# The first phase of a recurrent attention kernel, put in another order

## The chip, the cores and the metric

The kernel runs on one core of one Trainium2 chip. A core has five engines that run side by side, each through its own list of instructions in order: TensorE (PE, matmuls), VectorE (DVE), ScalarE (ACT), GpSimd (POOL), and SyncE (SP), which here does nothing but start DMAs. Engines wait for each other and for DMAs through semaphores. The metric is device time of one launch in microseconds, as the median of several runs.

## What is computed

Two layers in one launch. The first is a recurrence over time with a 40 x 40 state for each of 32 heads (4 batches of 8), over 768 positions; the second is a feed-forward layer with a bent square as its activation, on the 3072 rows that come out:

```python
for t in range(S):
    y[:, :, t] = np.einsum('bhd,bhde->bhe', rt, state)
    Sa = np.einsum('bhde,bhe->bhd', state, at)
    state_decay = state * wt[:, :, None, :] - np.einsum('bhd,bhe->bhde', Sa, bt)
    state = state_decay + np.einsum('bhd,bhe->bhde', vt, kt)
...
h = x @ w_in                       # 3072 x 320 by 320 x 2048
g = np.where(pos, h, np.where(neg, 0.0, (h + beta) ** 2 / (4.0 * beta)))
return g @ w_out                   # 3072 x 2048 by 2048 x 320
```

Inputs and results are float32; the weights come to the kernel as 64-bit integers whose two words together hold the double-precision number.

## The kernel before

**The recurrence in chunks.** 768 positions are 24 chunks (`c`) of 32, and each chunk has two halves (`hb`) of 16 heads. Inside a chunk the recurrence becomes small matrix products, one of which needs the inverse of a 32 x 32 triangular matrix per head. Four chunks make a set (`s`), of which there are six; a set's decay products, its scores and its inverses are worked out together.

**What a set needs before its chunks can run:**

- *Pair products* (`early_products` for sets 0 and 1, `prelude` for the later ones): running products of the decays and what follows from them, on VectorE and POOL. They leave `early_out[s]`, which lies in the buffers `wides[1]` for set 0 and `wides[0]` for set 1.
- *Rows in memory*: `early_store` writes these products, and `copy_rv` with `pad_scr` copies the inputs r and v, to a scratch tensor `scr[s]`. From it `load_ti` and `load_cg` (part 0) fetch the rows of one chunk half into `tih[hb]` and `cg`.
- *Scores for the inverse*: `early_turn` transposes the products with TensorE, and ScalarE copies them to `turned[s]`; `early_ab` multiplies them, copies the result (L206) and stores it to `abd[s]` in eight DMAs (L208).
- *The inverse* (`invert`): L316 loads `abd[s]` into `lw`; then 31 pairs of a multiply (L326) and a subtraction (L332), each dependent on the one before, on VectorE for set 0 and on POOL for later sets; L335 stores the inverse to `ttd[s]`, and `load_cg` part 1 (L409) fetches it for a chunk half. `step_back("inv", 0)` issues one further step of it.

**The chain of chunks.** `chain(c, hb)` begins with the matmuls of L463 and takes five steps (matmuls L463, L473, L491, transposes L520, matmuls L529, with VectorE and ScalarE work between them). `turn` transposes rows on VectorE, and `scores` works out in-chunk scores. The main loop calls `step` ten times for each chunk, alternating between halves. In the text a step is one such call, counted from the loop's start: chunk 1 begins at step 10, chunk 2 at step 20. With each step go two `pull(wgen, 2)` resumptions of the weight conversion, a piece of feed-forward work (`feed`), and the share of the later sets' preparation that is due by then (`background`, by the step windows in `WINDOWS`: the inverse of set 1 from step 16 to 36, the rows of set 2 from step 20 to 36).

**The feed-forward layer** (`moe`) works on groups of 64 positions, 12 in all. Group 0 is laid out after step 21 of the main loop, and its work is let in with a delay of five steps. A group goes through 16 blocks `f` of 128 hidden units; block `f` needs columns of `w_in` and rows of `w_out`. Its matmuls are L600, L574 and L578.

**The weight conversion** (`weights`, a generator called `wgen`) turns the 64-bit numbers into pairs of rounded floats. There are 28 jobs: 12 for `w_in` (`into`, 1024 words wide in the buffer) and 16 for `w_out` (`outof`, 640 words). A job has a load, a scaling on ScalarE (L681), three instructions on VectorE (L687, L716, L718), a cast on ScalarE (L694) and the split-off of the rest on POOL (L695). Two resumptions of the generator issue about one job. The raw numbers stay in lent buffers: `lending` lists which kinds may be used (5 and 6 are the two X tiles, 7 `lw`, 8 `arena`, 9 `tiab`, and before the change 1 for the two `tih` tiles and 2 for `Yraw`). `reclaim(kind)` takes a kind back: it resumes the generator until no job stands in it.

**The first phase** is everything ahead of the main loop. All DMAs in question stand in SP's one list, in the order in which the program issues them. Before the change the phase runs: loads for sets 0 and 1, first weight loads, products of set 0, transposes of set 0, products of set 1, weight loads and conversions between the two halves of the scores, the inversion of set 0. While the inversion's 62 instructions are issued one a step (`i`), a table `todo` adds other work at given `i`, and `rest` adds one DMA a step: stores of set 0, copies of r and v, stores of set 1. At every fifth `i` the conversion is resumed once.

Of the kernel before, what the change touches and what calls it, by code (L numbers as in the profile page):

```python
# [10 lines left out]
F32R = mybir.dt.float32r  # L11
# [38 lines left out]
def rwkv_moe_kernel(ctx: ExitStack, tc: tile.TileContext, r, k, v, w, a, b, w_in, w_out, ident_d, mask_d, out):  # L50
    nc = tc.nc
# [68 lines left out]
    def copy_rv(s, part, c):  # L120

        x, o = ((r, O_R), (v, O_V))[part]
        nc.sync.dma_start(
            scr4[s][c, :, :, o : o + D], x.rearrange("b h (n t) e -> (b h) n t e", t=L)[:, 4 * s + c]
        )

    def pad_scr(s):
        nc.sync.dma_start(scr[s][NH * 128 : NH * 128 + 1, 0:D], r[0, 0, 0:1, :])
# [6 lines left out]
    early_in = [[x.rearrange("p (t e) -> p t e", e=D) for x in xs] for xs in early_in]  # L135
    early_out = [x.rearrange("p (t x) -> p t x", x=160) for x in (wides[1], wides[0])]
    turned = [
        [cgf[i][:, 0:2048].rearrange("p (n t) -> p n t", t=L) for i in ij] for ij in ((0, 1), (2, 0))
    ]

    early_rows = {}
# [7 lines left out]
    def early_products(s):  # L149

        wl, al, bl, kl = early_in[s]
        R = early_out[s]
        kt, P, at, bt = (R[:, :, D * i : D * i + D] for i in range(4))
        rec = arena.rearrange("p (t e) -> p t e", e=D)
        seg = lambda x: x.rearrange("p (s t) e -> p s t e", t=8)
        Ps, ws, rs = seg(P), seg(wl), seg(rec)
        nc.vector.tensor_copy(Ps[:, 1:, 0], ws[:, 1:, 0])
        nc.vector.tensor_scalar(out=P[:, 0], in0=wl[:, 0], scalar1=-1.0, scalar2=None, op0=ALU.mult)
        for t in range(1, 8):
            nc.vector.tensor_mul(Ps[:, :, t], Ps[:, :, t - 1], ws[:, :, t])  # L160
        for i in range(1, 4):
            nc.vector.tensor_mul(Ps[:, i], Ps[:, i], Ps[:, i - 1, 7:8].broadcast_to([128, 8, D]))
        nc.gpsimd.tensor_scalar(out=at[:, 0], in0=al[:, 0], scalar1=-1.0, scalar2=None, op0=ALU.mult)
        for i in range(4):
            ts_ = slice(max(8 * i, 1), 8 * i + 8)
            nc.gpsimd.tensor_mul(at[:, ts_], al[:, ts_], P[:, max(8 * i, 1) - 1 : 8 * i + 7])
        nc.vector.reciprocal(rs[:, :, 7], Ps[:, :, 7])
        for t in range(7, 0, -1):
            nc.vector.tensor_mul(rs[:, :, t - 1], rs[:, :, t], ws[:, :, t])
        for i in range(4):  # L170
            ts_ = slice(8 * i, 8 * i + 8)
            nc.vector.tensor_mul(bt[:, ts_], bl[:, ts_], rec[:, ts_])
        for h in range(2):
            ts_ = slice(16 * h, 16 * h + 16)
            nc.gpsimd.tensor_mul(kt[:, ts_], kl[:, ts_], rec[:, ts_])

    def early_turn(s, j, part):

        for i in range(2):
            ps = psum().rearrange("p (t n) -> p t n", n=128)  # L180
            at = 8 * part + 4 * i
            for k in range(4):
                nc.tensor.transpose(ps[0:D, k, :], early_out[s][:, at + k, 80 + 40 * j : 120 + 40 * j], eye)
            for f in range(2):
                nc.scalar.copy(
                    turned[s][j][64 * f : 64 * f + D, :, at : at + 4].rearrange("e (p c) t -> e p c t", c=4),
                    ps[0:D].rearrange("e t (p f c) -> e f p c t", f=2, c=4)[:, f],
                )
# [24 lines left out]
    def early_store(s, c):  # L213

        nc.sync.dma_start(scr4[s][c, :, :, 80:240], early_out[s][c::4])
# [403 lines left out]
    def weights():  # L619
# [18 lines left out]
        def outof(f):  # L638
            ready_at[f] = len(jobs) + 1
            jobs.append(  # L640
                ([w_out[128 * f : 128 * f + 128, :]], f // 8, lambda f=f: (w2[f // 8][:, 0, f % 8], w2[f // 8][:, 1, f % 8]))
            )

        for j in range(4):
            into(j)
        for f in range(8):
            outof(f)
        for f in range(8, NF):
            outof(f)
        todo = list(range(len(jobs)))  # L650
        size = lambda k: (sum(x.shape[0] for x in jobs[k][0]), jobs[k][0][0].shape[1])

# [72 lines left out]
    def reclaim(kind):  # L725

        lending.discard(kind)
        while any(x[0] == kind for x in sts.values()):
            next(wgen)

    def pull(gen, n=1):
        for _ in range(n):
            if next(gen, "end") == "end":
                return False
        return True

    ready_in, ready_at, converted, w2 = {}, {}, [0], []
    needs = lambda f: max(ready_in[f], ready_at[f])
    lending, sts, room, loader = {1, 2, 5, 6, 7, 8, 9}, {}, [], []
    load = lambda q: loader[0](q)  # L740
    pair = lambda x: x.rearrange("p (a b) -> p a b", b=2)
    wgen = weights()
# [1 line left out]
    def step_back(key, s):  # L744
        if s < NS and done.get(key, -1) < s:
            next(back[key])
# [3 lines left out]
    for f in range(2):  # L750
        nc.sync.dma_start(ident[64 * f : 64 * f + 64], ident_d[64 * f : 64 * f + 64, 64 * f : 64 * f + D])
    nc.sync.dma_start(mask, mask_d)
    lend = lambda n, xs: room.extend((n, x.bitcast(I32)) for x in xs)
    lend(5, [Xraw[0]])
    lend(6, [Xraw[1]])
# [2 lines left out]
    for j in range(2):  # L758
        for k in range(4):
            early_turn(0, j, k)  # L760
    early_products(1)
    lend(1, [flat(x) for x in (tih[1], tih[0])])
    lend(9, [flat(tiab)])
    lend(8, [arena])
    load(nc.sync)
    pull(wgen, 2)
    early_ab(0, 0)
    pull(wgen, 2)
    early_ab(0, 1)
    step_back("inv", 0)  # L770
    lend(2, [Yraw])
    load(nc.sync)
    pull(wgen, 2)
    rest = []
    for c in range(4):
        rest += [lambda c=c: early_store(0, c)] + [lambda c=c, i=i: copy_rv(0, i, c) for i in range(2)]
    rest += [lambda: pad_scr(0)]
    rest += [lambda c=c: early_store(1, c) for c in range(4)]
    i = 0
    todo = {}  # L780
    at = lambda n, f: todo.setdefault(n, []).append(f)

    def reuse():

        reclaim(1)
        for x in tih:
            pad_rows(x, 168)
        for hb in range(2):
            load_ti(0, hb)
            load_cg(0, hb, (0,))  # L790

    def ahead(hb):
        for j in range(3):
# [4 lines left out]

    for j in range(2):
        for k in range(4):  # L800
            at(1 + 4 * j + k, lambda j=j, k=k: early_turn(1, j, k))
    at(9, lambda: early_ab(1, 0))
    at(10, lambda: early_ab(1, 1))
    at(14, lambda: w2.append(wide(1)))
    at(24, lambda: w2.append(wide(0)))
    for k in range(3):
        at(12 + 2 * k, lambda k=k: init_cg(k, 0))
        at(16 + 2 * k, lambda k=k: init_cg(k, 1))
    at(3, lambda: lending.discard(1))
    at(16, reuse)  # L810
    at(36, lambda: lending.discard(2))
    at(51, lambda: ahead(0))
    at(55, lambda: ahead(1))
    while done.get("inv", -1) < 0:
        step_back("inv", 0)
        i += 1
        for f in todo.pop(i, ()):
            f()
        if rest:
            rest.pop(0)()  # L820
        if i % 5 == 0:
            pull(wgen)
    assert not todo, todo
    lend(7, [lw])
    load(nc.sync)
    reclaim(2)
    Y.append(y_tile(F32R))
    for hb in range(2):
        load_cg(0, hb, (1,))
    jobs_done = [0]  # L830
    mgen = moe()
    gens = {}
# [107 lines left out]
```

## Time and profile before

| | us |
|---|---|
| median of 3 runs | 1017.51 |
| lowest and highest run | 1013.65, 1018.44 |
| the profiled execution | 1022.44 |
| its span, first to last instruction | 1020.6 |
| busy in the span: PE, POOL, DVE, ACT | 809.8, 583.5, 564.4, 529.9 |
| first chain matmul (L463) starts | 116.58 |
| granted TensorE clock, mean | 0.844 |

Times in the profile are microseconds from the span's start, durations in means are in ns. A group of instructions is named by line, engine and operation, with what it writes and reads. "Idle before" is time in which the engine waited just ahead of such an instruction, with the releaser. SPq rows are the issues of DMAs on SP. A busy engine may be one that stands in the middle of an instruction and is held up there, so equal instructions are compared by duration too.

### The profile page before, as it was taken

Reading aid. Unit: us, or ns where it says so; the run is one execution under the profiler, and the core shown is the slowest. Engines: PE = TensorE matmul, PEld = TensorE weight load, DVE = VectorE, ACT = ScalarE, POOL = GpSimd, SP = SyncE. Lnnn points to the kernel's source line nnn. Section 1 sums busy time; section 2 is a strip of 40 time slices with the busy share of each in tenths; the row PEclk is TensorE's granted clock in tenths of the full one; section 3 lists DMA queues with packets and bytes.
Section 4 is the critical chain, followed back from the end, with each engine's and each line's share of the span. In section 5 each row is a group of like instructions: output and inputs, shape, how many; then the busy total and the mean of one; then the engine's idle time right before and its main releaser. Section 6 shows DMA issues by size and latency. Waiting matters only on the chain.

```text
span 1020.6 us, 34597 instructions
## 1 busy us (share of the span) xinstructions
PE 809.8 (79%) x14240; PEld 725.4 (71%) x14240; DVE 564.4 (55%) x1432; ACT 529.9 (52%) x1326; POOL 583.5 (57%) x781
## 2 busy tenths in 40 slices
PE   4511375556988977899879898989999899999995
PEld 3311365445877966788778787868998789999995
DVE  7598388464555662774643675654554345455321
ACT  5671254213554543564455455546666466667663
POOL 4423354687452699543699544798346984434332
PEclk9755555667797889797888898989999899999998
DMA  6699694755587755885735885755755355443010
GB/s 249 165 216 234 160 220 103 167 109 127 128 172 142 157 135 118 165 174 124 165 87 111 180 172 123 154 122 119 134 115 116 85 105 89 111 77 73 12 43 14
DMA packets 276862, 134.56 MB, mean 132 GB/s; under 512 B 194984, under 2 KB 266856, under 8 KB 276704
## 3 DMA queue, kind: packets, MB, share of 16 engines
q1 hardware_dynamic: 273504, 121.20, 55.6%
q0 software_dynamic: 3200, 11.14, 3.6%
q8 instruction: 112, 1.84, 0.8%
q14 instruction: 46, 0.38, 0.1%
HBM read 96.83 MB, written 33.82 MB: 128 GB/s over the span
## 4 chain that ended last, share of the span: by engine, by line
PE 36%; POOL 19%; DMA 11%; DVE 9%; issue 8%; SPq 7%; ACT 4%; POOLq 0%; DVEq 0%; ACTq 0%
PE ph L600 11%; PE po L574 6%; POOL lw L326 5%; POOL lw L332 5%; DMA ti<-scr 4%; PE po L578 4%; PE p L473 3%; PE p L491 3%; POOL gl L588 3%; DMA ld_a<-in_a_dram 3%; POOL cg L447 3%; PE p L463 3%; SPq L274 2%; PE p L435 2%; DVE arena L243 2%
## 5 line engine op out<-in xcount | busy, mean ns | idle before, releaser
L600 PE MATMUL ph<-X,w 120*128 120x256 f32 x1536 | 263.1, 309 | 23.2 <-DVE qt L613 17.9
L588 POOL TENSOR_TENSOR gl<-qt,gh 128x256 fp32r<-128x256 f32 x192 | 140.4, 731 | 236.6 <-ACT gh L587 215.9
L600 PEld LDWEIGHTS ph<-X,w 120*128 120x128 f32 x1536 | 223.1, 206 | 39.3 <-DVE qt L613 21.4
L613 DVE SCALAR_TENSOR_TENSOR qt<-qt,ph 128x256 f32<-128x256 f32 x192 | 79.9, 416 | 172.5 <-ACT qt L607 166.3
L574 PE MATMUL po<-wide,gh 128*128 128x320 f32 x768 | 165.1, 332 | 0.4 <-ACT gh L587 0.4
L587 ACT CAST gh<-qt 128x256 fp32r<-128x256 f32 x192 | 78.0, 406 | 163.4 <-DVE qt L613 162.6
L447 POOL TENSOR_TENSOR cg<-cg,mask 32x512 f32<-32x512 f32 x96 | 121.8, 1269 | 32.5 <-ACT cg L445 26.5
L578 PE MATMUL po<-wide,gl 128*128 128x320 f32 x384 | 102.0, 344 | 43.7 <-POOL gl L588 43.7
L574 PEld LDWEIGHTS po<-wide,gh 128*128 128x128 f32 x768 | 126.5, 205 | 3.6 <-ACT gh L587 0.6
L606 ACT ACTIVATE qt<-ph,half_c 128x256 f32<-128x256 f32 x192 | 90.6, 472 | 74.0 <-POOL gl L588 67.4
L578 PEld LDWEIGHTS po<-wide,gl 128*128 128x128 f32 x384 | 66.8, 201 | 51.4 <-POOL gl L588 48.8
L326 POOL TENSOR_TENSOR lw<-lw 128x31 f32<-128x31 f32 (+15 forms) x155 | 93.5, 603 | 16.3 <-DMA lw<-abd 7.6
L484 ACT ACTIVATE cg<-p 32x160 f32<-32x160 f32 x192 | 56.8, 296 | 79.6 <-DVE cg L480 46.0
L480 DVE SCALAR_TENSOR_TENSOR cg<-p,mask 32x128 f32<-32x128 f32 x192 | 55.7, 290 | 71.2 <-PE p L473 46.8
L463 PE MATMUL p<-cg 128*64 128x72 f32 x1536 | 71.8, 254 | 25.8 <-issue 22.5
L435 PE MATMUL p<-cg,ev 40*32 40x32 f32 x1536 | 62.8, 202 | 32.9 <-DVE ev L423 31.9
L332 POOL TENSOR_TENSOR lw<-lw 128x31 f32<-128x31 f32 (+15 forms) x155 | 83.7, 540 | 8.8
L463 PEld LDWEIGHTS p<-cg 128*64 128x64 f32 x1536 | 63.5, 158 | 33.2 <-issue 29.1
L498 DVE SCALAR_TENSOR_TENSOR cg<-p,pr 40x160 f32<-40x160 f32 x184 | 59.0, 321 | 46.5 <-PE p L491 44.6
L435 PEld LDWEIGHTS p<-cg,ev 40*32 40x32 f32 x1536 | 56.6, 114 | 39.1 <-issue 32.1
L607 ACT ACTIVATE qt<-qt 128x256 f32<-128x256 f32 x192 | 80.1, 417 | 6.1
L491 PE MATMUL p<-cg 128*64 128x72 f32 (+1 forms) x1536 | 69.9, 251 | 16.1 <-ACT cg L484 8.6
(119 smaller groups left out, 1313.7 us busy)
## 6 DMA issues: line engine op xcount, KB each, us to landing
ti<-scr SPq DMA_DIRECT2D x96, 200.0 KB
ti<-scr SPq DMA_DIRECT2D x96, 168.0 KB
scr<-arena POOLq DMA_DIRECT2D x16, 640.0 KB, 5.3
cg<-scr SPq DMA_DIRECT2D x96, 80.0 KB
X<-Y SPq DMA_DIRECT2D x36, 160.0 KB
scr<-wide SPq DMA_DIRECT2D x8, 640.0 KB
tiab<-scr SPq DMA_DIRECT2D x32, 160.0 KB
scr<-in_r_dram SPq DMA_DIRECT2D x24, 160.0 KB
```

The source lines that it names most:

```text
L326: eng.tensor_mul(t3, W3[:, 0:n, j : j + 1].broadcast_to([128, n, m]), L3[:, j + 1 :, j].unsqueeze(1).broadcast_to([128, n, m]),)
L332: eng.tensor_sub(W3[:, 0:n, j + 1 :], W3[:, 0:n, j + 1 :], t3)
L435: nc.tensor.matmul(ps[q, p, 0:32], lhsT=ev[rows, p, 1, :], rhs=cg[rows, 2 * p + f, C_X : C_X + 32], start=True, stop=True,)
L447: nc.gpsimd.tensor_mul(o, o, mask[q].unsqueeze(1).unsqueeze(1).broadcast_to([32, 8, 2, 32]))
L463: nc.tensor.matmul(psv[h // 8][64 * (1 - f) : 64 * (1 - f) + 64, h // 2 % 4, 0:72], lhsT=cg[:, h, C_T : C_T + 64], rhs=cg[:, h, C_R : C_R ...
L491: nc.tensor.matmul(psv[h // 8][64 * f : 64 * f + 64, h // 2 % 4, 0:n3], lhsT=cgw[:, h * CW + C_G : h * CW + C_G + 64], rhs=cg[:, h, C_R : ...
L574: nc.tensor.matmul(pos[i], lhsT=gh[:, ts_], rhs=w2[f // 8][:, j, f % 8, :], start=f == 0 and j == 0, stop=False)
L578: nc.tensor.matmul(pos[i], lhsT=gl[:, ts_], rhs=w2[f // 8][:, 0, f % 8, :], start=False, stop=f == NF - 1)
L588: nc.gpsimd.tensor_sub(gl, gt, gh.bitcast(F32))
L600: nc.tensor.matmul(ph, lhsT=w1[:, wi, fs], rhs=Xs[g][:, xi, :], start=i == 0, stop=i == 7)
L606: nc.scalar.activation(gt, ph, AF.Relu, bias=half_c, scale=0.5)
L607: nc.scalar.activation(gt, gt, AF.Square)
```

## The change

The first phase is put in another order. The copies of r and v go to the head of SP's list, right behind the loads. The scores of set 0 and the start of its inversion come ahead of the products of set 1. Zeroing and padding, the stores of set 0 and the loads of the first rows stand ahead of the inversion's steps. The `tih` tiles and `Yraw` are not lent to weights any more, and `Yraw` takes a part of the turned values of set 1 that lay in `cgf[0]`. No conversion is resumed before the main loop; five jobs' loads are issued before the inversion's steps and three behind it. `ahead`, which turns the rows of chunk 0 and fetches those of chunk 1, moves from steps 51 and 55 of the inversion to 36 and 44. The fetch of the inverse is issued ahead of the weight loads into `lw`. The jobs of both layers alternate: three of `w_in`, then the four of `w_out` that go with them.

```diff
-        [cgf[i][:, 0:2048].rearrange("p (n t) -> p n t", t=L) for i in ij] for ij in ((0, 1), (2, 0))
+        [x[:, 0:2048].rearrange("p (n t) -> p n t", t=L) for x in xs] for xs in ((cgf[0], cgf[1]), (cgf[2], Yraw))
...
         for j in range(4):
             into(j)
-        for f in range(8):
-            outof(f)
-        for f in range(8, NF):
-            outof(f)
+            for f in range(4 * j, 4 * j + 4):
+                outof(f)
...
-    lending, sts, room, loader = {1, 2, 5, 6, 7, 8, 9}, {}, [], []
+    lending, sts, room, loader = {5, 6, 7, 8, 9}, {}, [], []
...
     nc.sync.dma_start(mask, mask_d)
+    for c in range(4):
+        for i in range(2):
+            copy_rv(0, i, c)
+    pad_scr(0)
...
     for j in range(2):
         for k in range(4):
             early_turn(0, j, k)
+    for half in range(2):
+        early_ab(0, half)
+    step_back("inv", 0)
     early_products(1)
-    lend(1, [flat(x) for x in (tih[1], tih[0])])
+    for k in range(2):
+        init_cg(k, 0)
+    for x in tih:
+        pad_rows(x, 168)
+    for k in range(2):
+        init_cg(k, 1)
+    for c in range(4):
+        early_store(0, c)
+    for hb in range(2):
+        load_ti(0, hb)
+        load_cg(0, hb, (0,))
     lend(9, [flat(tiab)])
     lend(8, [arena])
     load(nc.sync)
-    pull(wgen, 2)
-    early_ab(0, 0)
-    pull(wgen, 2)
-    early_ab(0, 1)
-    step_back("inv", 0)
-    lend(2, [Yraw])
-    load(nc.sync)
-    pull(wgen, 2)
-    rest = []
-    for c in range(4):
-        rest += [lambda c=c: early_store(0, c)] + [lambda c=c, i=i: copy_rv(0, i, c) for i in range(2)]
-    rest += [lambda: pad_scr(0)]
-    rest += [lambda c=c: early_store(1, c) for c in range(4)]
+    rest = [lambda c=c: early_store(1, c) for c in range(4)]
...
-            at(1 + 4 * j + k, lambda j=j, k=k: early_turn(1, j, k))
-    at(9, lambda: early_ab(1, 0))
-    at(10, lambda: early_ab(1, 1))
-    at(14, lambda: w2.append(wide(1)))
-    at(24, lambda: w2.append(wide(0)))
-    for k in range(3):
-        at(12 + 2 * k, lambda k=k: init_cg(k, 0))
-        at(16 + 2 * k, lambda k=k: init_cg(k, 1))
-    at(3, lambda: lending.discard(1))
-    at(16, reuse)
-    at(36, lambda: lending.discard(2))
-    at(51, lambda: ahead(0))
-    at(55, lambda: ahead(1))
+            at(2 + 4 * j + k, lambda j=j, k=k: early_turn(1, j, k))
+    at(13, lambda: early_ab(1, 0))
+    at(14, lambda: early_ab(1, 1))
+    at(16, lambda: init_cg(2, 0))
+    at(17, lambda: init_cg(2, 1))
+    at(36, lambda: ahead(0))
+    at(44, lambda: ahead(1))
     while done.get("inv", -1) < 0:
         step_back("inv", 0)
         i += 1
         for f in todo.pop(i, ()):
             f()
-        if rest:
+        if rest and i > 8:
             rest.pop(0)()
-        if i % 5 == 0:
-            pull(wgen)
     assert not todo, todo
+    for hb in range(2):
+        load_cg(0, hb, (1,))
+    for i in (1, 0):
+        w2.append(wide(i))
+    Y.append(y_tile(F32R))
     lend(7, [lw])
     load(nc.sync)
-    reclaim(2)
-    Y.append(y_tile(F32R))
-    for hb in range(2):
-        load_cg(0, hb, (1,))
```

(`reuse`, which is removed with its entry, padded `tih` and loaded the first rows after taking kind 1 back.)

More of the change, by code (lines that the diff above doesn't have):

```diff
@@ L781, in rwkv_moe_kernel @@
     at = lambda n, f: todo.setdefault(n, []).append(f)
[L783 to L787, printed above, removed]
-        for hb in range(2):
-            load_ti(0, hb)
-            load_cg(0, hb, (0,))
     def ahead(hb):
@@ L818, in rwkv_moe_kernel @@
             f()
-        if rest:
+        if rest and i > 8:
             rest.pop(0)()
-        if i % 5 == 0:
-            pull(wgen)
     assert not todo, todo
+    for hb in range(2):
[3 more added lines that the diff above has]
+    Y.append(y_tile(F32R))
     lend(7, [lw])
     load(nc.sync)
-    reclaim(2)
-    Y.append(y_tile(F32R))
-    for hb in range(2):
-        load_cg(0, hb, (1,))
     jobs_done = [0]
```

## The prediction

> **What bounds the kernel now.** I read the busy time by stages (a row gives the stretch, then each engine's busy us with its instruction count, the granted TensorE clock, the DMA share and GB/s), then the DMA queue's rows in order of time, and last VectorE's groups.
>
> ```profile
> 20.00:28.50 8.50, 5.05 (x269) 4.18 (x267) 7.85 (x18) 3.61 (x9) 3.99 (x5) 0.85 0.13 41
> ...
> 32.70:48.50 15.80, 8.61 (x48) 5.29 (x48) 5.26 (x11) 12.53 (x31) 6.92 (x5) 0.68 0.67 171
> 48.50:97.60 49.10, 9.26 (x389) 8.02 (x388) 44.46 (x89) 22.90 (x36) 13.47 (x16) 0.51 1.09 231
> 97.60:116.60 19.00, 0.02 (x1) 0.05 (x1) 5.16 (x8) 2.41 (x4) 4.65 (x4) 0.50 0.91 195
> 116.60:132.80 16.20, 11.57 (x204) 10.70 (x205) 10.55 (x24) 8.49 (x21) 7.52 (x8) 0.50 0.63 146
> 132.80:148.60 15.80, 11.16 (x206) 9.94 (x201) 14.73 (x30) 8.62 (x22) 7.94 (x8) 0.50 1.00 213
> 148.60:164.00 15.40, 10.04 (x188) 9.04 (x190) 14.19 (x29) 8.74 (x22) 8.03 (x8) 0.61 0.63 135
> 164.00:177.00 13.00, 7.19 (x141) 6.66 (x139) 11.00 (x20) 5.60 (x14) 8.34 (x9) 0.50 0.56 115
> 177.00:190.00 13.00, 5.58 (x150) 4.94 (x147) 3.32 (x15) 3.16 (x8) 5.95 (x12) 0.63 0.68 136
> ...
> 700.00:800.00 100.00, 97.68 (x2007) 88.70 (x2007) 52.90 (x144) 64.08 (x164) 58.80 (x87) 0.98 0.61 122
> ```
>
> Late on TensorE is the bound (97.68 of 100 us). Before the first chain matmul (116.6) it has 9.26 us of work in 49 and then nothing for 19. From 48.5 to 97.6 VectorE is busy 44.46 of 49.10 us, and so it is in the first chunks (14.73 of 15.80, 14.19 of 15.40). So up to 177 VectorE sets the pace. Everything behind is issued in the order of the steps, which the change leaves alone, so what the first chunks gain moves the end one for one.
>
> **First phase.** These rows (start, duration) carry the present chain from scores to first matmul.
>
> ```profile
> 29.57 0.67 ACT L681 ACTIVATE ti<-ti 80x512 f32<-80x512 f32 x1 [5.83 <-DMA ti<-in_moe_w_in_dram]
> 35.48 0.60 ACT L206 COPY ea<-p 128x512 f32<-128x512 f32 x1
> ...
> 25.84 1.55 PE L202 MATMUL p<-cg,cg 40*32 40x32 f32 x103 [1.89 <-issue]
> ...
> 34.33 2.28 SPq L208 DMA_DIRECT2D abd<-ea  x4
> 39.97 2.43 SPq L208 DMA_DIRECT2D abd<-ea  x4
> 50.10 4.62 SPq L123 DMA_DIRECT2D scr<-in_v_dram  x1
> 93.38 10.05 SPq L274 DMA_DIRECT2D ti<-scr  x8
> 103.71 0.34 SPq L335 DMA_DIRECT2D ttd<-lw  x1
> 104.49 7.96 SPq L667 DMA_DIRECT2D lw<-in_moe_w_out_dram  x3
> ...
> 116.58 2.49 PE L463 MATMUL p<-cg 128*64 128x72 f32 x32 [22.55 <-issue]
> ...
> 48.51 0.21 DVE L326 TENSOR_TENSOR lw<-lw 128x31 f32<-128x31 f32 x1 [10.55 <-DMA lw<-abd]
> ...
> 96.25 1.32 DVE L332 TENSOR_TENSOR lw<-lw 128x31 f32<-128x31 f32 x1
> ```
>
> *Start of the inversion.* The score matmuls of set 0 end at 27.4, but their copies stand behind weight scalings on ScalarE, one of which waited 5.83 for its load, and their stores behind weight loads on SP: the last store is out at 42.4, and VectorE starts at 48.5, 6.1 later. Afterwards both obstacles stand behind. Copies end by 28.0, eight stores at 2.35 per four are out by 32.7 at most, or 30.5 if the first four go while the second half is multiplied; I take 31, so a start at 37. Ahead of them on SP then stand eight r and v copies and the pad; 20.00:28.50 shows a DMA share of 0.13, room to hide them. If that cover fails they cost about one such slow issue (4.62), a start at 42; 34 if the copies wait for nothing. The products of set 1 end on VectorE where they end now (the cut at 32.70 is their end), so they do not delay it.
>
> *Length.* VectorE's groups from 48.5 to 97.6 (count | busy us, mean ns | idle before), and two equal multiplies with POOL beside the second:
>
> ```profile
> L326 DVE TENSOR_TENSOR lw<-lw 128x31 f32<-128x31 f32 (+15 forms) x31 | 16.2, 524 | 11.4 <-DMA lw<-abd 10.6
> L332 DVE TENSOR_TENSOR lw<-lw 128x31 f32<-128x31 f32 (+15 forms) x31 | 11.9, 383 | 1.0
> ...
> L420 DVE STREAM_TRANSPOSE cg<-ti 64x256 f32<-64x256 f32 x4 | 1.8, 438 | 2.8 <-DMA ti<-scr 2.8
> ...
> L423 DVE STREAM_TRANSPOSE ev<-ti 128x512 f32<-128x512 f32 x2 | 1.4, 711 | 0.0
> ...
> L425 DVE STREAM_TRANSPOSE pr<-ti 128x512 f32<-128x512 f32 x2 | 1.3, 668 | 0.0
> ...
> 56.59 0.54 DVE L326 TENSOR_TENSOR lw<-lw 128x220 f32<-128x220 f32 x1
> ...
> 77.04 1.50 DVE L326 TENSOR_TENSOR lw<-lw 128x220 f32<-128x220 f32 x1
> ...
> 76.86 1.29 POOL L695 TENSOR_TENSOR w<-X,w 120x512 fp32r<-120x512 f32 x1 [0.95 <-ACT w L694]
> ```
>
> The inversion itself is 16.2 + 11.9 = 28.1; with the transposes of `ahead` (4.5) and the same 2.8 of waiting for rows it is 35.4. About 3 goes with the weight splits that stretched it (1.50 instead of 0.54, and the last pair). So 32.5 instead of 49.1, and it ends at 69.5. The rows are loaded earlier too: stores of set 0 follow the inversion's load on SP, so `ti` should land near 52, when step 36 asks for it.
>
> *Tail.* Now 97.57 to 116.58, 19.0: 6.1 until SP has issued the next rows (the 10.05 row), then 12.9 from the store of the inverse to the matmul. Three weight loads inside that go behind the four `cg<-ttd` issues, but the landing of the store remains: I take 10. SP is what is late next, with the second set's stores, the scores' eight and the next rows behind each other: 5. Together 15, so the chain starts at 84.5. **First phase: -32.** Bounds: start 34 and a tail of 9.5, chain at 76, -40; start 42 and a tail of 18, chain at 92.5, -24.
>
> **What is pushed into the loop.** Busy time of L687, L716 and L718, the three VectorE instructions of a conversion job, one pair of rows each, before the chain and in its first 61 us; then L695, POOL's split, in the latter:
>
> ```profile
> 30.00:116.60 86.60, 9.27 (x12) 0.56 0.95 210
> 116.60:178.00 61.40, 15.13 (x16) 0.53 0.70 154
> ...
> 30.00:116.60 86.60, 8.04 (x11) 0.56 0.95 210
> 116.60:178.00 61.40, 9.36 (x17) 0.53 0.70 154
> ...
> 30.00:116.60 86.60, 7.48 (x11) 0.56 0.95 210
> 116.60:178.00 61.40, 10.53 (x17) 0.53 0.70 154
> ...
> 116.60:178.00 61.40, 19.49 (x19) 0.53 0.70 154
> ...
> 33.27 0.42 DVE L716 TENSOR_SCALAR X<-X 120x512 uint32<-120x512 uint32 x1
> 33.60 0.68 DVE L687 SCALAR_TENSOR_TENSOR X<-X 120x512 f32<-120x512 f32 x1
> 34.20 0.68 DVE L718 SCALAR_TENSOR_TENSOR X<-X 120x512 uint32<-120x512 uint32 x1
> ```
>
> Of the 28 jobs eleven have had their VectorE work before the chain: 9.27 + 8.04 + 7.48 = 24.8 us. Afterwards no `pull` stands there, so all 24.8 comes into the loop, beside the 35.0 already there. The loop pulls one job a step, as now. By the lists of free buffers 16 jobs are through at step 16, where the inversion of set 1 wants `lw` back and forces six at once; the last falls at step 21. Today the last falls at step 16. The next chunk's chain starts at step 20.
>
> Up to 177 VectorE is busy 10.55 + 14.73 + 14.19 + 11.00 = 50.5 of 60.4: 9.9 idle, some 4 of it before the first chain product is there. I let 5 be filled. **Loop: +20.** Clean, a job costs 1.78 by the three rows (11 x 1.78 = 19.6), and with all idle filled and the 9.7 idle of 177 to 190 too, nothing is left: +0. With a 1.29 split blocking each job, 11 x 3.07 = 34 and nothing filled: +34. I stay near the 24.8 because that row has the very same jobs, stalls included. POOL has 19 of the 28 splits in the loop now and gets nine more, 11.6 by the 1.29, on 31.8 busy of 60.4: no bound.
>
> The Trainium skill speaks against the change here: SBUF — State Buffer, Who interferes with whom, says that a VectorE instruction with two SBUF inputs contends with a GpSimd instruction that reads SBUF, and that the second to issue blocks until the first is through. The 1.50 beside 0.54 agrees. By the page the splits taken off the inversion stall the chain's stage instead, a loop nearer the +34; without it, nearer +15.
>
> **Other edits.** The rows' buffers and `Y` are no longer lent, which removes waits on SP and adds none; `Yraw` instead of `cgf[0]` holds turned values, no instruction more. Zeroing and padding move to ScalarE before step 1, beside the inversion's start (ScalarE busy 12.53 of 15.80 there): cost nothing, or some 3 if the rows then wait for the pads. Alternating both layers' jobs changes no count, and all are done before the feed-forward begins some five steps after step 22.
>
> **Sum.** -32 + 20 = -12. A check through VectorE: 105.4 busy between 32.7 and 177 (5.26 + 44.46 + 5.16 + 50.5), less 3, plus idle of 4.3 before the inversion, 2.8 in it, 15 + 4 around the chain's start, 5 in the loop, ends at 32.7 + 133.5 = 166, 11 earlier than 177. The profiled execution took 1022.44 us, so 1010.4; the median of the three runs is 1017.51, 4.9 under it, and I forecast from that: **1005.5 us**, own range 997 to 1012.
>
> **Rivals.**
> - *The conversions hide.* Chain and conversion wait on different things and the idle of the loop takes 18 of the 24.8: -32 + 7 = -25, **992**. For it: 9.9 + 9.7 idle up to 190. Against: 14.73 of 15.80.
> - *The gain is all paid back.* The six forced jobs and longer stalls fill the loop to +30, or the first phase stays bound by DMA (share 1.09 now) and gives -24 against +22: about **1016**, no change.
> - *Slower: a job's stages run in series in the chain.* Scale 0.67 on ScalarE (the L681 row) and a cast of the same tile taken as equal, 1.78 on VectorE, split 1.29 on POOL are 4.4 us; eleven of them 48, less 5 filled: +43 - 32 = +11, **1028**. It decides from (32 + 5) / 11 = 3.4 us of delay per moved job. Against it: the loop now digests a job in some 3 us, its chain step included (61.40 for 19 splits).
>
> **How the numbers follow.** Forecast 0.5, hidden 0.2, paid back 0.18, slower 0.12. A measurement of this kernel can tell about 0.5% from no change, 5 us: faster means under 1012.4, slower over 1022.6. Faster is 0.5 and 0.2, less a little of the forecast's upper edge: 0.69; same 0.19; slower 0.12. The range leaves out the lower end of "hidden" and nearly all of "slower": 989 to 1020.
>
> **What would show it.** The inversion's first multiply near 37, its last near 69.5, first L463 near 84.5, start of the chain's fifth unit (step 20) near 165 instead of 177. L687, L716 and L718 with no instruction before the chain, and about 60 us of them behind it. Should VectorE be far from full from 85 to 165, the hidden case holds; should the first L463 come after 100, the DMA queue was the bound and my first phase is wrong. Should the last third not keep its pace, the one-for-one shift is wrong.

## The result, and the profile after

| | before | after |
|---|---|---|
| median of 4 runs (us) | 1017.58 | 1004.43 |
| lowest and highest run | 1013.65, 1018.44 | 1003.35, 1006.21 |
| the profiled execution, its span | 1022.44, 1020.6 | 1003.35, 1001.6 |
| granted TensorE clock, mean | 0.844 | 0.861 |
| first chain matmul starts | 116.58 | 84.36 |
| ScalarE's first copy in the chain's fifth unit (step 20) | 178.35 | 167.64 |

The ratio of the medians is 0.988, interval 0.985 to 0.991: 13 us faster, against a forecast of 1005.5. The profiled execution of before was slower than all its timed runs and that of after is the fastest of its own, so that pair lies 19 us apart; whatever the traces show beyond 13 us is not safely the change's.

The edits shift line numbers behind them by two: L681, L687, L716, L718, L694 and L695 of before are now L679, L685, L714, L716, L692 and L693.

Busy time by stages after, in the columns of the prediction's first fence (stretch, then PE, PEld, DVE, ACT and POOL with counts, granted clock, DMA share, GB/s):

```profile
37.30:72.10 34.80, 16.41 (x432) 12.65 (x432) 32.68 (x70) 18.94 (x42) 5.51 (x5) 0.60 1.08 243
72.10:84.40 12.30, 0.04 (x1) 0.07 (x2) 0.01 (x1) 0.00 (x0) 0.00 (x0) 0.50 0.82 178
84.40:97.00 12.60, 7.56 (x116) 7.11 (x118) 8.80 (x19) 7.37 (x16) 3.79 (x3) 0.64 0.80 186
97.00:114.50 17.50, 10.47 (x207) 9.61 (x205) 16.03 (x31) 8.82 (x21) 10.65 (x10) 0.60 0.99 213
114.50:132.00 17.50, 9.89 (x203) 9.12 (x201) 15.32 (x30) 8.74 (x22) 11.38 (x10) 0.60 0.90 186
132.00:166.00 34.00, 12.81 (x243) 11.56 (x240) 28.66 (x55) 16.52 (x36) 23.95 (x19) 0.55 0.58 153
```

The inversion (first row) is shorter by 14 us and VectorE is at least as full in it as before (32.68 of 34.80 us, 44.46 of 49.10). The second row, the tail, holds hardly any work on an engine, only DMA. Then VectorE is busy 8.80 + 16.03 + 15.32 + 28.66 = 68.8 of 81.6 us up to 166; before it was 50.5 of 60.4.

The rows that carry the first phase, from the timeline (start, duration; an SPq row is a series of issues):

```profile
24.84 6.76 SPq L208 DMA_DIRECT2D abd<-ea  x8
...
56.71 7.14 SPq L215 DMA_DIRECT2D scr<-wide  x4
64.39 7.44 SPq L208 DMA_DIRECT2D abd<-ea  x8
71.93 3.93 SPq L274 DMA_DIRECT2D ti<-scr  x8
75.96 0.40 SPq L335 DMA_DIRECT2D ttd<-lw  x1
82.52 1.78 SPq L409 DMA_DIRECT2D cg<-ttd  x4
...
37.29 0.21 DVE L326 TENSOR_TENSOR lw<-lw 128x31 f32<-128x31 f32 x1 [4.61 <-DMA lw<-abd]
...
71.90 0.21 DVE L332 TENSOR_TENSOR lw<-lw 128x31 f32<-128x31 f32 x1
...
84.36 2.55 PE L463 MATMUL p<-cg 128*64 128x72 f32 x32 [20.50 <-DMA cg<-ttd]
```

The eight stores of the scores are out at 31.6, the inversion runs from 37.29 to 72.1. Its last result then waits for SP, which issues the second set's stores and scores and the next rows until 75.9; the inverse is stored at 75.96, its fetch can go only 6.5 us later, and the first matmul follows 1.8 behind that.

In the loop the burst at step 16, where the inversion of set 1 takes `lw` back, is the one thing that stands out (of after: first waits between 134 and 168, each as the waiting instruction, its releaser, and the us in total, the times and the longest; then the timeline):

```profile
PE p L491 <- DVE cg L480: 15.8, 1, 15.8
ACT X L679 <- DMA X<-in_moe_w_in_dram: 5.8, 2, 4.3
```

```profile
143.65 6.82 POOL L693 TENSOR_TENSOR w<-X,w 120x512 fp32r<-120x512 f32 x2
...
133.81 0.70 ACT L468 COPY x<-p 128x288 f32<-128x288 f32 x2
167.64 0.70 ACT L468 COPY x<-p 128x288 f32<-128x288 f32 x2
```

TensorE stands 15.8 us at L491 for a product that VectorE owes it (L480), because the forced conversions are ahead of it in VectorE's list. Fourth to fifth unit takes 33.8 us (the last two rows); before it took 178.35 - 162.74 = 15.6.

### The profile page after: what moved, and what is told of

The parts are those of the page before. It is cut to its first block, busy times and chain, and to the rows that moved or that the text cites. A ratio compares the mean times of both kernels' runs of the same rounds, so it can differ in the third digit from the quotient of the medians.

```text
span 1001.6 us, 34605 instructions
## 1 busy us (share of the span) xinstructions
PE 800.1 (80%) x14240; PEld 715.5 (71%) x14240; DVE 569.4 (57%) x1432; ACT 530.5 (53%) x1326; POOL 588.2 (59%) x781
## 4 chain that ended last, share of the span: by engine, by line
PE 41%; POOL 17%; DVE 16%; DMA 11%; issue 6%; ACT 4%; SPq 4%; POOLq 0%; DVEq 0%; ACTq 0%
PE ph L600 12%; PE po L574 6%; POOL lw L326 4%; POOL lw L332 4%; PE po L578 4%; PE p L463 4%; PE p L473 3%; PE p L491 3%; POOL cg L447 3%; POOL gl L588 2%; DMA ti<-scr 2%; DVE rec L252 2%; PE p L435 2%; DVE arena L243 2%; PE p L439 2%
## 5 line engine op out<-in xcount | busy, mean ns | idle before, releaser
L600 PE MATMUL ph<-X,w 120*128 120x256 f32 x1536 | 258.5, 305 | 26.4 <-DVE qt L613 20.3
L600 PEld LDWEIGHTS ph<-X,w 120*128 120x128 f32 x1536 | 218.9, 202 | 42.7 <-DVE qt L613 24.2
L574 PE MATMUL po<-wide,gh 128*128 128x320 f32 x768 | 161.7, 326 | 0.3 <-ACT gh L587 0.3
L447 POOL TENSOR_TENSOR cg<-cg,mask 32x512 f32<-32x512 f32 x96 | 122.5, 1276 | 38.9 <-ACT cg L445 16.4
L574 PEld LDWEIGHTS po<-wide,gh 128*128 128x128 f32 x768 | 122.8, 199 | 3.6 <-ACT gh L587 0.5
L578 PEld LDWEIGHTS po<-wide,gl 128*128 128x128 f32 x384 | 65.9, 198 | 51.5 <-POOL gl L588 49.1
L491 PE MATMUL p<-cg 128*64 128x72 f32 (+1 forms) x1536 | 71.0, 253 | 33.0 <-DVE cg L480 33.0
L491 PEld LDWEIGHTS p<-cg 128*64 128x64 f32 x1536 | 63.0, 158 | 42.3 <-ACT cg L484 33.7
L480 DVE SCALAR_TENSOR_TENSOR cg<-p,mask 32x128 f32<-32x128 f32 x192 | 55.7, 290 | 57.3 <-PE p L473 31.6
L463 PE MATMUL p<-cg 128*64 128x72 f32 x1536 | 68.5, 249 | 21.1 <-DMA cg<-ttd 20.5
L463 PEld LDWEIGHTS p<-cg 128*64 128x64 f32 x1536 | 61.1, 154 | 28.2 <-issue 24.2
L498 DVE SCALAR_TENSOR_TENSOR cg<-p,pr 40x160 f32<-40x160 f32 x184 | 59.1, 321 | 33.5 <-PE p L491 31.6
L445 ACT COPY cg<-p 32x512 f32<-32x512 f32 x96 | 55.3, 576 | 33.4 <-PE p L439 31.9
```

What stands on the lines that cost most here:

```text
L447: nc.gpsimd.tensor_mul(o, o, mask[q].unsqueeze(1).unsqueeze(1).broadcast_to([32, 8, 2, 32]))
L463: nc.tensor.matmul(psv[h // 8][64 * (1 - f) : 64 * (1 - f) + 64, h // 2 % 4, 0:72], lhsT=cg[:, h, C_T : C_T + 64], rhs=cg[:, h, C_R : C_R ...
L491: nc.tensor.matmul(psv[h // 8][64 * f : 64 * f + 64, h // 2 % 4, 0:n3], lhsT=cgw[:, h * CW + C_G : h * CW + C_G + 64], rhs=cg[:, h, C_R : ...
L574: nc.tensor.matmul(pos[i], lhsT=gh[:, ts_], rhs=w2[f // 8][:, j, f % 8, :], start=f == 0 and j == 0, stop=False)
L578: nc.tensor.matmul(pos[i], lhsT=gl[:, ts_], rhs=w2[f // 8][:, 0, f % 8, :], start=False, stop=f == NF - 1)
L600: nc.tensor.matmul(ph, lhsT=w1[:, wi, fs], rhs=Xs[g][:, xi, :], start=i == 0, stop=i == 7)
```

## The experiments

Times are medians, ratios are against before on the same chip (where it had 1015 to 1018 us). A unit starts where ScalarE's first copy of it (L468) starts. Units 1 and 5 are the first chunk's half 0 and the third's.

| kernel | median | ratio, interval | unit 1 | unit 4 | unit 5 | unit 6 |
|---|---|---|---|---|---|---|
| before | 1017.58 | | 118.15 | 162.74 | 178.35 | 199.03 |
| after | 1004.43 | 0.988, 0.985 to 0.991 | 85.99 | 133.81 | 167.64 | 190.54 |
| e4_store1 | 998.68 | 0.983, 0.977 to 0.989 | 78.62 | 127.43 | 160.46 | 183.12 |
| e3_inv6 | 998.26 | 0.983, 0.977 to 0.989 | 87.29 | 134.57 | 160.40 | 182.70 |
| e1_tail6 | 996.35 | 0.981, 0.976 to 0.986 | 86.16 | 133.77 | 159.62 | 181.43 |
| e9_pull3 | 1001.40 | 0.987, 0.982 to 0.992 | 85.83 | 148.07 | 165.48 | 186.69 |
| e5_nosplit | 991.54 | 0.977, 0.974 to 0.980 | 85.16 | 128.83 | 157.35 | 178.00 |
| e2_order | 1024.42 | 1.008, 1.005 to 1.010 | 85.64 | 138.35 | 165.50 | 205.91 |
| e12_order_pull3 | 999.25 | 0.985, 0.981 to 0.988 | 85.78 | 149.76 | 164.32 | 186.61 |
| e13_before_alt | 1031.84 | 1.018, 1.014 to 1.021 | 138.91 | 185.16 | 192.44 | 214.16 |
| e10_tail_store | 997.13 | 0.984, 0.980 to 0.989 | 79.08 | 131.92 | 159.45 | 181.41 |
| e11_tail_store_pull3 | 992.38 | 0.978, 0.974 to 0.982 | 80.10 | 147.12 | 157.79 | 178.56 |

All but e13 are edits of the kernel after. Only e5_nosplit, e11, e2_order and e13 have an interval clear of that of after. For the others a gain over after rests on the medians and on the unit starts of one trace each; every run of theirs but those of e9 lies under the lowest of after.

### What the tail waits for

**e4_store1** takes the second set's stores out of the inversion's steps; the loop issues them.

```diff
         for f in todo.pop(i, ()):
             f()
-        if rest and i > 8:
-            rest.pop(0)()
     assert not todo, todo
```

> The changed kernel with the four stores of set 1's products (640 KB each) moved from the inversion's steps to the first four steps of the main loop. DMA theory of the tail (12.3 us from the inversion's end to the chain, of which 6.5 for the store of the inverse to land behind queued transfers): the store lands in 3 to 4 us and SP is free earlier, the chain starts at 78 to 81 instead of 84.4, median near 1000. Rival: the stores meet the row and weight loads of the first units, which come later by as much; the chain starts earlier but the fifth unit stays near 166, median 1003 to 1006.

From its timeline:

```profile
63.19 4.82 SPq L274 DMA_DIRECT2D ti<-scr  x8
...
72.49 0.34 SPq L335 DMA_DIRECT2D ttd<-lw  x1
75.13 1.78 SPq L409 DMA_DIRECT2D cg<-ttd  x4
...
76.98 2.57 PE L463 MATMUL p<-cg 128*64 128x72 f32 x32 [12.68 <-DMA cg<-ttd]
```

The store of the inverse leaves 3.5 us earlier, and its fetch can go 2.6 us after it instead of 6.5. The chain starts 7.4 earlier, the fifth unit 7.2, and the run is 5.8 shorter. So the tail is DMA: SP's list, and a landing behind what was issued ahead.

What it lands behind looks to be the loads of the next rows (L274) rather than the second set's stores. The fetch of the inverse goes 82.52 - 75.86 = 6.7 us after SP has issued these loads in after, and 75.13 - 68.01 = 7.1 here, where none of the set's product stores stands ahead; in e10 and e11 below it is 6.8 and 6.6. The stores then cost time by making SP issue the row loads late. This is inferred from the rows: no run moved the row loads alone.

**e3_inv6** puts six resumptions of the conversion among the inversion's last steps.

```diff
         if rest and i > 8:
             rest.pop(0)()
+        if i in (46, 49, 52, 55, 58, 61):
+            pull(wgen)
     assert not todo, todo
```

> The changed kernel with six conversion resumptions inside the last 20 steps of the inversion instead of behind it. VectorE theory: three jobs are 6 us on VectorE, which stretch the inversion: it ends near 78 instead of 72, the chain starts near 90, the loop is 6 us shorter, median 1003 to 1006. Should the chain's start be set by DMA alone (the store of the inverse landing), the chain starts near 84 to 86 and the median is near 999, as with the resumptions behind the inversion.

```profile
79.48 0.20 DVE L332 TENSOR_TENSOR lw<-lw 128x31 f32<-128x31 f32 x1
...
79.71 0.33 SPq L335 DMA_DIRECT2D ttd<-lw  x1
83.72 1.81 SPq L409 DMA_DIRECT2D cg<-ttd  x4
```

The inversion ends at 79.7 instead of 72.1, yet the first copy of unit 1 is only 1.3 later, because SP is free by then and the fetch can go 4.0 us after the store. Up to some 7 us at the end of the inversion are as good as free: as the kernel after stands, it is DMA and not the inversion's end that sets the chain's start. The fifth unit comes 7.2 earlier, with three jobs gone from the loop.

### Whether VectorE's work is what the loop pays

**e1_tail6** puts the same six resumptions into the idle tail.

```diff
     Y.append(y_tile(F32R))
+    pull(wgen, 6)
     lend(7, [lw])
     load(nc.sync)
```

> The changed kernel with six conversion resumptions (jobs 0 to 2 of 28) issued between the end of the inversion and the chain, where every engine is idle from 72 to 84 us. VectorE theory (the loop is paid for by VectorE's conversion work, wherever it stands): some 6 us of VectorE work leave the loop, the chain still starts near 84, the fifth unit comes some 6 us earlier than 166, median near 998.5. Burst theory (the loop is paid for by the jobs forced at step 16, which wait for each other and for loads): 13 resumptions are forced there instead of 11, the distance between the fourth and fifth unit stays at 34 us, median 1003 to 1005.

The tail by stages, in the columns of the first fence:

```profile
72.30:84.60 12.30, 0.01 (x1) 0.04 (x1) 6.46 (x15) 1.76 (x3) 5.71 (x2) 0.50 0.83 177
```

Chain start (84.59) and unit 4 do not move, the fifth unit comes 8.0 earlier, and the median is 8.1 lower. Fourth to fifth unit takes 25.9 us, so the burst theory fails. VectorE did 6.46 us in the tail. But from the first chain matmul to the fifth unit its busy time falls by only 4.4 (70.41 to 65.98 us), and its idle time by 3.8 (12.8 to 9.0). So three jobs taken out of the loop come back as 8 us, of which VectorE's own work is about half; the other half is waiting that went with the jobs.

**e9_pull3** resumes the conversion three times a step instead of twice: the same work, but spread, with less left for the burst.

```diff
             if k == 0:
-                pull(wgen, 2)
+                pull(wgen, 3)
```

> The changed kernel with three conversion resumptions a step of the main loop instead of two. By the lists of free buffers 2 resumptions are then forced at step 16 instead of 11 and none at step 20; the last job falls at step 18 instead of 21. VectorE theory: the same 28 jobs on VectorE before the fifth unit, units one to four come later by what the burst loses, fifth unit within 3 us of 166, median 1003 to 1006. Buffer theory (a forced job waits for its own load, since SP can issue that only when POOL has split an earlier job out of the buffer; the burst's 18 us are partly that wait): without the burst the waits spread, fifth unit 5 to 9 us earlier, median 995 to 999.

```profile
84.00:166.00 82.00, 43.18 (x754) 38.52 (x754) 76.66 (x142) 44.62 (x100) 52.60 (x48) 0.51 0.77 180
```

Between 84 and 166 VectorE is busy 76.7 of 82 us; the long stand is gone, units 2 to 4 are late instead, and the fifth comes 2.2 earlier, as the VectorE theory had it. The median, 1001.40, lies between the ranges of the two theories. The 33.8 us between units 4 and 5 of after look like the place of the loss, but by these starts only 2 to 4 us of them (the sixth unit comes 3.9 earlier) belong to the burst. The rest is time that VectorE takes for the jobs before step 20, wherever it takes it. Not all of it is work: the three conversion instructions of all 28 jobs take 22.37 + 17.26 + 22.52 = 62.2 us here, against the 58.5 of after (rows below).

**e5_nosplit** replaces POOL's split of all 28 jobs by a fill, which reads nothing; the second parts of the weights are left out of the computation.

```diff
             nc.scalar.copy(hi, x)
-            nc.gpsimd.tensor_sub(lo, x, hi.bitcast(F32))
+            nc.gpsimd.memset(lo.bitcast(F32), 0.0)
```

> The changed kernel with the weights' second parts left out: POOL writes zeros there (a memset) instead of the subtraction of the 28 jobs, so that POOL reads nothing for them. Contention theory (VectorE's conversion instructions stand while POOL splits, by 0.7 to 1.1 us a job): VectorE's time for the 28 jobs falls from some 60 us to 40, the loop up to the fifth unit by 10 to 18 us, median 987 to 995. If VectorE's stretched instructions only fill time in which it would wait anyway: the fifth unit moves by under 4 us, median above 1000.

VectorE's conversion time from 72 to 182 (stretch, busy us with count, clock, DMA share, GB/s), the three instructions L685, L714 and L716 of all 28 jobs, first of after:

```profile
72.00:182.00 110.00, 22.04 (x28) 0.56 0.76 171
72.00:182.00 110.00, 13.42 (x28) 0.56 0.76 171
72.00:182.00 110.00, 23.03 (x28) 0.56 0.76 171
```

and the same of e5_nosplit:

```profile
72.00:182.00 110.00, 18.44 (x28) 0.55 0.81 188
72.00:182.00 110.00, 12.56 (x28) 0.55 0.81 188
72.00:182.00 110.00, 18.63 (x28) 0.55 0.81 188
```

58.5 us become 49.6 with the same instructions on the same data: 8.9 us of VectorE's time in after were stalls beside the splits. The fifth unit comes 10.3 earlier, the run is 12.9 shorter. From the first chain matmul to the fifth unit VectorE is busy 61.13 of 73.95 us, in after 70.41 of 83.20: busy time and length fall alike, by 9.3, which is the best evidence that VectorE's time is what the loop pays. (POOL is busy 21 us less there too and may free buffers sooner, but VectorE's idle time stays at 12.8.) The contention theory had expected some 40 us and not 49.6; what holds up the rest was not followed. The rule of the Trainium skill that the prediction quoted (SBUF — State Buffer, Who interferes with whom) adds that a GpSimd instruction that only writes does not contend; this pair agrees in direction, by 58.5 against 49.6.

### The order of the jobs

**e2_order** undoes the alternation alone: all jobs of `w_in` first.

```diff
         for j in range(4):
             into(j)
-            for f in range(4 * j, 4 * j + 4):
-                outof(f)
+        for f in range(NF):
+            outof(f)
```

> The changed kernel with all twelve w_in jobs ahead of the sixteen w_out jobs, as before the change. By the lists of free buffers 3 resumptions are forced at step 16 instead of 11, and 8 at step 20 instead of 2; the number of jobs is the same. VectorE theory: the same work, so the fifth unit within 3 us of 166 and the median 1002 to 1006. Burst theory: the distance between the fourth and fifth unit falls from 34 us to 20 to 24; what step 20 gives back is hidden where VectorE waits for the rows of set 2, median 994 to 999.

It is 20 us slower than after and slower than before, which no theory had. Up to the fifth unit nothing is lost (165.50); the sixth is 40.4 later, in after 22.9. The stages there, and ScalarE's scalings with the loads they wait for:

```profile
165.00:206.00 41.00, 8.45 (x129) 7.58 (x131) 21.97 (x48) 9.70 (x26) 19.39 (x27) 0.50 0.42 99
```

```profile
159.78 0.49 ACT L679 ACTIVATE X<-X 128x320 f32<-128x320 f32 x1 [4.10 <-DMA X<-in_moe_w_out_dram]
164.62 0.48 ACT L679 ACTIVATE X<-X 128x320 f32<-128x320 f32 x1 [3.96 <-DMA X<-in_moe_w_out_dram]
170.27 0.48 ACT L679 ACTIVATE tiab<-tiab 128x320 f32<-128x320 f32 x1 [4.07 <-DMA tiab<-in_moe_w_out_dram]
176.72 0.48 ACT L679 ACTIVATE arena<-arena 128x320 f32<-128x320 f32 x1 [5.60 <-DMA arena<-in_moe_w_out_dram]
181.86 0.48 ACT L679 ACTIVATE X<-X 128x320 f32<-128x320 f32 x1 [4.29 <-DMA X<-in_moe_w_out_dram]
```

No engine is full, and the DMA share is 0.42. Scalings follow each other at (181.86 - 159.78) / 4 = 5.5 us, each behind its own load: set 2 wants `arena` back from step 20 on, and the jobs up to the last one that stands in it are forced through one after the other, load included. Meanwhile TensorE is busy 8.45 of 41 us. This is the serial course of the prediction's slower rival, at another place and with each job's load in series too, which the rival's 4.4 us a job left out.

**e12_order_pull3** tests that reading: the same order, but three resumptions a step, so that fewer jobs are left to be forced (the edits of e2_order and e9_pull3 together).

```diff
         for j in range(4):
             into(j)
-            for f in range(4 * j, 4 * j + 4):
-                outof(f)
+        for f in range(NF):
+            outof(f)
...
             if k == 0:
-                pull(wgen, 2)
+                pull(wgen, 3)
```

> The changed kernel with all w_in jobs first and three resumptions a step. With two resumptions this order took 1024 us, since 8 were forced at step 20 with lw and arena both withdrawn, one job every 5 to 6 us. Now none is forced at either step. Buffer theory: the order itself costs nothing, the 20 us come back wholly, median 995 to 1003, fifth and sixth unit as with the alternating order and three resumptions. Rival (the order costs by itself, through wider loads early or through later readiness): median 1012 or more.

All of e2's loss comes back: 999.25, unit 5 to 6 takes 22.3. The order as such costs nothing; jobs left over when their buffers are withdrawn cost it.

**e13_before_alt** puts the alternation alone into the kernel before.

```diff
         for j in range(4):
             into(j)
-        for f in range(8):
-            outof(f)
-        for f in range(8, NF):
-            outof(f)
+            for f in range(4 * j, 4 * j + 4):
+                outof(f)
```

> The kernel before the change with the alternating order of jobs alone. VectorE theory: the jobs that go ahead of the chain are then a mixture of both layers; nine w_out jobs at some 1.2 to 2 us of VectorE time and twelve w_in jobs at 1.8 to 2.9 change places, which moves some 3 to 6 us of VectorE work out of the first phase into the loop; both are bound by VectorE, so no change, 1013 to 1021. If the alternation is a gain or a loss by itself, the median lies more than 5 us from 1017.

17 us slower than before on the same chip, where the VectorE theory had expected no change, and the chain starts at 137.5 instead of 116.58. Its inversion, by stages and in the timeline:

```profile
48.40:121.80 73.40, 8.57 (x384) 7.68 (x384) 49.05 (x96) 26.26 (x44) 16.75 (x19) 0.51 0.85 188
```

```profile
71.22 0.64 SPq L215 DMA_DIRECT2D scr<-wide  x1
...
75.42 0.47 ACT L692 CAST wide<-ti 128x320 fp32r<-128x320 f32 x1 [9.99 <-issue]
...
79.87 0.69 DVE L685 SCALAR_TENSOR_TENSOR X<-X 120x512 f32<-120x512 f32 x1 [13.28 <-ACT X L679]
```

VectorE has 49.05 us of work there, but the stretch is 73.4 instead of 49.1 long. The first `w_out` jobs write into `wide` tiles, one of which holds the products of set 0 until they are stored (71.22); the cast into it stands 10 us, and VectorE 13.28 behind it. That the cast waits for the store's read is inferred, since the profile names no releaser here. Another 9.21 us VectorE waits for a scaling of `ti` (L679, at 64.94), which follows 5.0 us of zero fills on ScalarE; together that is 22.5 of the 24.4 us that it stands idle. So the alternation loses 17 in the old arrangement and, at two resumptions a step, is worth 20 in the new one.

### A version that beats both

**e11_tail_store_pull3** takes e1_tail6, e4_store1 and e9_pull3 together; **e10_tail_store** is the same without the third.

```diff
-        if rest and i > 8:
-            rest.pop(0)()
...
     Y.append(y_tile(F32R))
+    pull(wgen, 6)
     lend(7, [lw])
...
             if k == 0:
-                pull(wgen, 2)
+                pull(wgen, 3)
```

> Three edits of the changed kernel at once: six resumptions behind the inversion, the stores of set 1's products moved into the loop, three resumptions a step. Each by itself: first -8 us (measured), second -6 us (measured), third -5 to -9 by the buffer theory or 0 by the VectorE theory. If they add, 1004.4 - 8 - 6 = 990 with the third at 0, and 982 to 986 with it. They add less if the tail, shorter by 7 us through the stores, has no room left for the 8 us of conversion on VectorE: 991 to 995.

> The changed kernel with six resumptions behind the inversion and the stores of set 1's products in the loop, two resumptions a step. VectorE theory: VectorE is full from the chain's start to the fifth unit whatever the number of resumptions a step, so this equals the kernel with all three edits: fifth unit 156 to 160, median 991 to 995. If the burst at step 16 (13 resumptions here) costs something of its own, the fifth unit comes 3 to 6 us later than the 157.8 there and the median is 995 to 998.

e11 gives 992.38, ratio 0.978 (0.974 to 0.982): 12 us under after, 24 under before on the same chip, and the lowest median of the kernels that do the whole computation, though its interval overlaps that of e1. The three gains do not add (8 + 6 + 3 would be 17). The expectation had the number for that case, but not the reason: the shorter tail does have room. VectorE does its conversions there from 72.42 to 78.80 in e10 and from 72.38 to 78.76 in e1, and in e10 it then stands idle for 4.6 us. What differs is the loop. From the first chain matmul to the fifth unit e10 takes 82.15 us with VectorE busy 67.90, e1 75.00 with 65.98, and ScalarE's scalings (L679) wait 26.9 us for weight loads in e10 and 10.5 in e1. That is the rival that the expectation of e4 named, stores in the way of loads, though in e4 itself the scalings wait no longer than in after (9.6 and 10.0). Why the loads come late was not tested.

e10 gives 997.13. Its unit 5 is as early as e1's and its interval overlaps both e1's and e11's, so what the third edit is worth there stays open.

## Why the prediction held

**Start of the inversion.** Forecast 37, measured 37.29: the last store of the scores out at 31.6 against 31, VectorE 5.7 behind it against 6.1. The room for the copies of r and v at the list's head was there.

**Its length.** Forecast 32.5, measured 34.8. The term that failed is "about 3 goes with the weight splits". Of the stretched instructions that it rests on, only the multiply at 77.04 (1.50 instead of 0.54) stands beside a split. The last pair stands beside POOL's mask products of the scores (L447), as these rows of before show:

```profile
94.97 1.24 DVE L326 TENSOR_TENSOR lw<-lw 128x31 f32<-128x31 f32 x1
...
94.72 2.77 POOL L447 TENSOR_TENSOR cg<-cg,mask 32x512 f32<-32x512 f32 x2 [2.42 <-ACT cg L445]
```

So about 1 us went with the splits, and the mask products stayed. They now fall beside longer instructions of the inversion; of after:

```profile
62.74 1.43 DVE L326 TENSOR_TENSOR lw<-lw 128x192 f32<-128x192 f32 x1
64.21 1.30 DVE L332 TENSOR_TENSOR lw<-lw 128x192 f32<-128x192 f32 x1
65.55 1.40 DVE L326 TENSOR_TENSOR lw<-lw 128x175 f32<-128x175 f32 x1
66.98 1.29 DVE L332 TENSOR_TENSOR lw<-lw 128x175 f32<-128x175 f32 x1
...
62.54 5.53 POOL L447 TENSOR_TENSOR cg<-cg,mask 32x512 f32<-32x512 f32 x4 [14.80 <-issue]
...
42.08 0.50 DVE L326 TENSOR_TENSOR lw<-lw 128x192 f32<-128x192 f32 x1
42.61 0.36 DVE L332 TENSOR_TENSOR lw<-lw 128x192 f32<-128x192 f32 x1
41.20 0.46 DVE L326 TENSOR_TENSOR lw<-lw 128x175 f32<-128x175 f32 x1
41.70 0.34 DVE L332 TENSOR_TENSOR lw<-lw 128x175 f32<-128x175 f32 x1
```

Four instructions take 5.42 beside POOL; equal ones without it take 0.50 + 0.36 + 0.46 + 0.34 = 1.66. That is 3.8 us of stretch where I had taken 3 away. The multiplies and subtractions take 16.1 + 12.5 = 28.6 instead of the forecast 25.1; some 1.8 of short gaps between instructions were not in the sum, and the 2.8 of waiting for rows that were in it did not come, which hides about half of the error. As e3_inv6 shows, the longer inversion cost the chain next to nothing.

**The tail.** Forecast 15 (5 for SP, 10 from store to matmul), measured 12.3 (3.9 and 8.4). The mechanism, SP's list and the landing, is shown by e4_store1. Inversion and tail are off by +2.3 and -2.7, so it is partly luck that the chain's start, forecast 84.5, was measured at 84.36. First phase: -32 forecast, -32.2 measured.

**The loop.** Forecast +20, from 24.8 us of VectorE's work less 5 of filled idle time. Measured by the unit starts: unit 1 to 5 took 60.2 and takes 81.65, +21.4. The three conversion instructions stand wholly behind the chain's start, with 58.5 us in all, as forecast (about 60). But the terms were off against each other here too. VectorE's conversion time between the chain's start and 166 (L685, L714, L716 of after):

```profile
84.40:166.00 81.60, 19.91 (x25) 0.58 0.77 178
84.40:166.00 81.60, 12.20 (x25) 0.58 0.77 178
84.40:166.00 81.60, 21.04 (x24) 0.58 0.77 178
```

That is 53.2 against 35.0, so 18.1 came in and not 24.8; the last few jobs fall behind 166. And no idle time was filled: it is 81.6 - 68.8 = 12.8 instead of 9.9, since in the burst VectorE itself waits for loads and scalings. 18.1 + 2.9 = 21, so the near hit of +20 is luck in its parts. That the jobs moved into the loop are the price is shown by e1_tail6 and e3_inv6: three jobs out of it bring the fifth unit 8.0 and 7.2 forward. That VectorE's time is the greater part of the price is supported by e5_nosplit, where both fall by 9.3, and by e9_pull3, where spreading the jobs leaves the fifth unit nearly in place. It is not the only limit: in e2_order, e13_before_alt and e10 the time goes where VectorE waits for buffers and loads.

**The alternation of the jobs.** The prediction put it at nothing, because it "changes no count". The count was right and the price was not: in e2_order the same change without the alternation takes 1024 us, and no term of the sum prices the order. That the version forecast at 1005.5 was the one with its forced jobs at step 16, where they cost 2 to 4 us, and not at step 20, where they cost 20, is luck as far as the prediction goes.

**POOL is no bound.** True for the stretch as a whole (3.79 + 10.65 + 11.38 + 23.95 = 49.8 busy of 81.6). But its reads stall VectorE: the two splits of 6.82 us in the burst and the 8.9 us of e5_nosplit fit one conflict seen from two sides. I weighed the contention only between +15 and +34 for the loop; without the splits' reads the loop takes 157.35 - 85.16 = 72.2, +12 against before.

**The rivals.** "The conversions hide" needed the loop's idle time on VectorE to be filled, and it grew from 9.9 to 12.8 us. "Paid back" needed +30 in the loop or a chain start at 92.5. The slower rival's mechanism exists: in e2_order jobs run in series at 5.5 us each, and the kernel lands at 1024. In after something like it is seen only in the burst.

**One for one to the end.** Fifth unit -10.7, medians -13.2; the sum was -12. The edits of after bear it out roughly: but for e2_order, whose loss comes behind it, their medians follow their fifth units within 3 us. Within the profiled pair the lead does not simply carry through. It falls to 8.1 us at the eighth unit, grows to 19.3 by the 28th (646.44 and 627.18) and then stays within 1 us of that to the last, so the last third keeps its pace and the middle does not. The two profiled executions lie 4.9 above and 1.1 below their medians, which would cover 6 of the 8 us; the granted clock was 0.844 and 0.861 over the whole span. What moves the middle was not separated.

## What to carry to other kernels

Work that is moved off one critical stretch into a loop is free only as far as the engine that does it has idle time there: sum that engine's busy time over the loop first, and move the work into a stretch where it waits for a DMA instead, as e1_tail6 does. A long wait in one place can be work that is merely late; spread it and see whether the end of the loop moves before calling the place the cause. When buffers are lent to a pipeline, count how many jobs are left when they are withdrawn: the same jobs in another order cost 20 us here, because the rest ran in series.

## What the hardware showed unexpectedly

- VectorE and POOL hold each other up in both directions: equal VectorE instructions took 1.43 and 0.50 us with and without POOL's mask products beside them, and in the burst two POOL splits, 1.29 us apiece in the prediction's row, took 6.82 together beside a VectorE that was nearly full.
- The fetch behind the same store of the inverse could go 2.6, 4.0 or 6.5 us after it (e4_store1, e3_inv6, after). With the row loads as the last issue ahead of the store, it went 6.6 to 7.1 us after SP had issued these loads, whenever the store itself was issued (after, e4_store1, e10, e11).
